# A recurrence and an MLP on one core: from hand-woven step lists to a source-level list scheduler with a shared PSUM pool and a one-function gelu

## The chip, the cores and the metric

The kernel runs on one core of one Trainium2 chip. The metric is device time in microseconds (us). The kernel before took 1344.1 us, the median of three runs (1341.94 to 1348.6).

## The reference, cut to what matters

Two parts follow each other. A recurrence over 768 steps with a 40x40 state for each of 4 x 8 heads gives `y`; its output, laid out as 3072 tokens x 320, goes through an MLP with a quick gelu. All of it is fp32, and the MLP weights arrive as fp64.

```python
for t in range(S):                                   # S = 768, D = 40
    y[:, :, t] = np.einsum('bhd,bhde->bhe', rt, state)
    Sa = np.einsum('bhde,bhe->bhd', state, at)
    state_decay = state * wt[:, :, None, :] - np.einsum('bhd,bhe->bhde', Sa, bt)
    state = state_decay + np.einsum('bhd,bhe->bhde', vt, kt)
# x: 3072 x 320, w_in: 320 x 2048, w_out: 2048 x 320
h = x @ w_in
g = h * (1.0 / (1.0 + np.exp(-1.702 * h)))
return (g @ w_out).astype(np.float32)
```

## The kernel before

The recurrence is done in chunks of 64 steps: 12 chunks x 2 pairs of batches = 24 units. In a unit a triangular system is solved by six "levels" of small matmuls, for two halves. Matmuls come in sets of four, one for each 64x64 quarter of the TensorE array (`QUARTERS` in the source; the page prints 64*64). Each chunk gives 256 tokens, and the MLP of a chunk is sixteen bursts of work: eight "ups" (into the gelu) and eight quarters of "downs". A level, with its four identity matmuls at the end, is

```python
for j in BITS:
    o = j * 168
    for h, t in QUARTERS:
        mm(ps[HALF[t], h, o + lo:o + 104], w[HALF[h], t, j, 104:], w[HALF[h], t, j, lo:104], j == 0)
    if hi == 168:
        for h, t in QUARTERS:
            mm(ps[HALF[t], h, o + 104:o + 168], w[HALF[h], t, j, :64], w[HALF[h], t, j, 104:], False)
view = ps[:, :, :336].rearrange("p h (j n) -> p h j n", n=168)
for h, t in QUARTERS:
    mm(view[HALF[t], h, :, 64:104], ident[HALF[h]], w[HALF[h], t, :, 64:104], False)
```

The order is made by hand. `weave` runs the steps of one unit's solve and slips in a share of a side list (preparation of the next unit, and the MLP of two chunks ago). PSUM, the memory that the matmuls write their results to, is held as four pairs of banks (four tiles of 128x2x512 fp32). They are split by purpose: one pair of banks for everything small, two for the levels, one for the MLP. The gelu is a sigmoid on ScalarE and a multiply on VectorE.

```python
ps_misc  = ... tile_pool(name="ps_misc",  bufs=1, space=bass.MemoryType.PSUM)
ps_solve = ... tile_pool(name="ps_solve", bufs=2, space=bass.MemoryType.PSUM)
ps_mlp   = ... tile_pool(name="ps_mlp",   bufs=1, space=bass.MemoryType.PSUM)
# [... cut ...]
nc.scalar.activation(sg, ph[:, :, :256], ACT.Sigmoid, scale=1.702)
nc.vector.tensor_mul(g, ph[:, :, :256], sg)
# [... cut ...]
if j < 0:                                   # the first two chunks: convert the weights instead
    mlp = weights[len(weights) * i // lead:len(weights) * (i + 1) // lead]
else:
    mlp = down(j) if p else up(j)           # MLP of chunk j = this one - 2
weave(solve(i), mixed(*[l for l in (side, mlp) if l]))
```

## Time and profile before

| what | value |
|---|---|
| median time | 1344.1 us |
| TensorE busy (matmul, PE) | 76% of the span |
| VectorE (DVE) / ScalarE (ACT) / GpSimd (POOL) busy | 32% / 23% / 16% |
| TensorE instructions (matmuls + weight loads) | 32416 + 32416 |
| mean granted TensorE clock (share of full speed) | 0.896 |

The lines of the three stages, the chain and the waits are in the prediction below. The first line is from the page's list of DMA queues (packets, MB, share of 16 engines' span). The second is the chain of waits by engine: the work that ended last, followed back step by step to what released it, as shares of the span. The third is one stretch of 100 us from the middle (stretch, its length, busy time with instruction counts of PE, PE weight load, DVE, ACT and POOL, granted clock, DMA share, GB/s).

```profile
q8 instruction: 254, 4.16, 1.3%
...
PE 64%; DVE 13%; ACT 8%; issue 7%; DMA 5%; POOL 3%; SPq 1%; POOLq 0%; DVEq 0%; ACTq 0%
```

TensorE has 2 x 32416 = 64832 instructions: each matmul that the kernel writes is two matmul and two weight-load records in the trace (an up, written as 20, is 40 + 40).

### The profile page before, as it was taken

The page shows a single profiled execution, that of the slowest core. Times are in us where ns is not written, and L with a number is a line of the kernel's source. Part 1 is how long each engine was busy: PE and PEld are TensorE (multiplying, and loading weights), DVE is VectorE, ACT ScalarE, POOL GpSimd, SP SyncE. Part 2 cuts the span into 40 slices and gives each one's busy share as a digit, 9 for nine tenths or more (in the row PEclk, how much of TensorE's full clock was granted, in tenths as well). Part 3 has the DMA queues.
Part 4 walks back from the last instruction along what each step waited for, and adds up shares of the span by engine and source line. Part 5 has one row for each costly group of instructions (what it writes and reads, how often), then busy time and mean ns, then how long its engine had stood idle before and what let it go on. Part 6 is the DMA issues. An engine that isn't in the chain of part 4 may idle for free.

```text
span 1348.7 us, 67403 instructions
## 1 busy us (share of the span) xinstructions
PE 1030.6 (76%) x32416; PEld 822.6 (61%) x32416; DVE 425.2 (32%) x823; ACT 313.9 (23%) x594; POOL 214.1 (16%) x238
## 2 busy tenths in 40 slices
PE   4666658787787887887887887877878878878677
PEld 3656547666666665765665665766666756665443
DVE  2676573222222322321321321322322322231110
ACT  2131212222221231231231231221321322211110
POOL 2666572001001001010010010001000100100000
PEclk9886677898997997998899898989989989899999
DMA  3233230101101101101101000110110110100000
GB/s 124 61 97 114 93 119 3 43 9 57 43 9 57 43 9 57 43 8 39 40 26 49 25 36 8 58 43 9 58 43 8 58 43 9 48 3 13 1 11 11
DMA packets 22544, 54.91 MB, mean 41 GB/s; under 512 B 2816, under 2 KB 14080, under 8 KB 22272
## 3 DMA queue, kind: packets, MB, share of 16 engines
q1 hardware_dynamic: 22272, 50.61, 11.9%
q8 instruction: 254, 4.16, 1.3%
q14 instruction: 18, 0.15, 0.0%
HBM read 46.66 MB, written 3.93 MB: 38 GB/s over the span
## 4 chain that ended last, share of the span: by engine, by line
PE 64%; DVE 13%; ACT 8%; issue 7%; DMA 5%; POOL 3%; SPq 1%; POOLq 0%; DVEq 0%; ACTq 0%
PE ps_down L530 17%; PE ps_up L512 16%; PE ps_level L94 11%; DMA in_chan<-in_chan 4%; PE ps_cum L94 3%; DVE W L318 3%; ACT sg L515 3%; PE ps_turn L94 2%; PE ps_N L94 2%; DVE g L517 2%; PE ps_y L94 2%; PE ps_saT L94 2%; PE ps_Av L94 1%; PE ps_RV L94 1%; PE ps_Z L94 1%
## 5 line engine op out<-in xcount | busy, mean ns | idle before, releaser
L512 PE MATMUL ps_up<-xT,w_in_sb 64*64 64x256 f32 x3840 | 250.0, 403 | 23.0 <-DVE g L517 20.2
L530 PE MATMUL ps_down<-w_out_sb,g 64*64 64x320 f32 x3072 | 255.0, 472 | 5.4 <-DVE g L517 2.9
L94 PE MATMUL ps_level<-W 64*64 64x64 f32 (+2 forms) x8448 | 227.5, 243 | 21.3 <-issue 10.9
L94 PEld LDWEIGHTS ps_level<-W 64*64 64x64 f32 x8448 | 209.9, 143 | 39.8 <-issue 13.1
L512 PEld LDWEIGHTS ps_up<-xT,w_in_sb 64*64 64x64 f32 x3840 | 160.9, 145 | 81.0 <-DVE g L517 26.6
L530 PEld LDWEIGHTS ps_down<-w_out_sb,g 64*64 64x64 f32 x3072 | 141.6, 149 | 76.5 <-issue 17.4
L517 DVE TENSOR_TENSOR g<-ps_up,sg 128x512 f32<-128x512 f32 x96 | 66.2, 690 | 260.6 <-ACT sg L515 260.6
L480 POOL TENSOR_TENSOR x<-y,F 64x320 f32<-64x320 f32 x24 | 20.4, 851 | 636.2 <-DVE y L475 636.0
L408 DVE COPY W<-ps_level 128x672 f32<-128x672 f32 (+1 forms) x120 | 96.0, 800 | 78.2 <-PE ps_level L94 77.8
L515 ACT ACTIVATE sg<-ps_up 128x512 f32<-128x512 f32 x96 | 57.4, 597 | 269.8 <-PE ps_up L512 269.8
L94 PE MATMUL ps_level<-W,ident 64*64 64x80 f32 x2304 | 107.5, 242 | 2.7 <-issue 2.5
L408 ACT COPY W<-ps_level 128x672 f32<-128x672 f32 (+1 forms) x120 | 81.3, 677 | 121.2 <-PE ps_level L94 117.8
L94 PEld LDWEIGHTS ps_level<-W,ident 64*64 64x64 f32 x2304 | 73.5, 143 | 3.6 <-issue 3.6
L94 PE MATMUL ps_xT<-ident,x 64*64 64x64 f32 x960 | 32.5, 262 | 37.7 <-POOL x L480 23.7
L171 POOL TENSOR_SCALAR scale<-scale 128x256 int32<-128x256 int32 (+1 forms) x36 | 47.3, 1315 | 66.1 <-DVE scale L170 65.9
L94 PEld LDWEIGHTS ps_xT<-ident,x 64*64 64x64 f32 x960 | 26.6, 168 | 44.0 <-POOL x L480 26.2
L535 ACT COPY ob<-ps_down 128x320 f32<-128x320 f32 x24 | 10.2, 426 | 182.7 <-PE ps_down L530 182.7
L278 POOL TENSOR_TENSOR ah<-in_time,F 128x320 f32<-128x320 f32 x24 | 23.4, 975 | 181.5 <-DMA in_time<-in_time 101.0
L332 POOL TENSOR_TENSOR RV<-RV,upper 128x512 f32<-128x512 f32 x24 | 30.5, 1272 | 131.8 <-ACT RV L331 131.6
L172 POOL TENSOR_SCALAR scale<-scale 128x256 int32<-128x256 int32 (+1 forms) x36 | 47.8, 1329 | 3.0
L94 PE MATMUL ps_RV<-in_chan 64*64 64x64 f32 x768 | 20.9, 262 | 33.4 <-DMA in_chan<-in_chan 31.5
L94 PE MATMUL ps_saT<-ident,sa 64*64 64x64 f32 x768 | 21.4, 257 | 28.5 <-DVE W L318 23.5
(103 smaller groups left out, 1204.1 us busy)
## 6 DMA issues: line engine op xcount, KB each, us to landing
in_time<-in_time SPq DMA_DIRECT2D x24, 800.0 KB, 5.0
in_chan<-in_chan SPq DMA_DIRECT2D x24, 512.0 KB, 6.0
raw<-in_w_in SPq DMA_DIRECT2D x40, 128.0 KB, 3.0
raw<-in_w_out SPq DMA_DIRECT2D x16, 320.0 KB, 3.0
in_w<-in_w SPq DMA_DIRECT2D x24, 160.0 KB, 6.4
out<-ob SPq DMA_DIRECT2D x48, 80.0 KB, 2.2
```

The costliest lines, as they stand in the source:

```text
L94: nc.tensor.matmul(o, lhsT, rhs, start=start, stop=True, skip_group_check=True)
L171: nc.gpsimd.tensor_scalar(scale, scale, 896.0, 0.0, ALU.subtract, ALU.max)
L172: nc.gpsimd.tensor_scalar(scale, scale, 255.0, 2.0 ** 23, ALU.min, ALU.mult)
L278: nc.gpsimd.tensor_mul(s["ah"][:, :, :D], by_head(a_b), by_head(Fs[i]))
L318: nc.vector.tensor_tensor(s["W"][b][:, :, :, o:o + 64], ps[:, :, b * 128:b * 128 + 128].rearrange("p e (f t) -> p e f t", t=64), mask.unsq ...
L332: nc.gpsimd.tensor_mul(s["RV"], s["RV"], upper8)
L408: copy(W[b][:, :, :, lo:], view[:, :, :, lo:])
L480: nc.gpsimd.tensor_mul(x[HALF[0]], y[HALF[0]], F[HALF[0]])
L512: nc.tensor.matmul(ph[HALF[h], r, :256], w_in_sb[HALF[r], k, m, h * 64:(h + 1) * 64], xTs[j][HALF[r], k, :], start=k == 0, stop=k == NK - 1)
L515: nc.scalar.activation(sg, ph[:, :, :256], ACT.Sigmoid, scale=1.702)
L517: nc.vector.tensor_mul(g, ph[:, :, :256], sg)
L530: nc.tensor.matmul(po[p][HALF[b], r, :DM], gTs[j][f // 2][HALF[r], f % 2, o:o + 64], w_out_sb[HALF[r], f, :], start=f == 0, stop=f == NF - 1)
```

## The change

The intent is to let no engine stand still while work is ready. All steps become small tasks with a rank, fixed durations and declared buffers. `Plan.order()` runs a list scheduler in the source that decides, once, the order on each engine. Four PSUM pairs form one pool. The gelu becomes one ScalarE function. Masks and multiplies leave GpSimd for VectorE, copies go to whichever of ScalarE and VectorE is free in the plan, and the weight conversion is rewritten: six VectorE operations a piece instead of five, one GpSimd operation instead of two.

```diff
+class Plan:
+    DELAY = {"PE": 330.0, "DVE": 130.0, "ACT": 130.0, "POOL": 150.0, "SP": 100.0}
+    def order(self):
+        def fits(t):
+            if t.pair is None or t.pair in held:
+                return True
+            clear = sum(p <= now for p in pairs)
+            return clear > 0 if t.most is None else clear > 1 and len(many) < t.most
+        while coming or able:
+            able.sort(key=lambda t: (t.rank, t.n))
+            # [... first task that fits on the first free engine; cut ...]
 [... cut ...]
-    ps_misc = ctx.enter_context(tc.tile_pool(name="ps_misc", bufs=1, space=bass.MemoryType.PSUM))
-    ps_solve = ctx.enter_context(tc.tile_pool(name="ps_solve", bufs=2, space=bass.MemoryType.PSUM))
-    ps_mlp = ctx.enter_context(tc.tile_pool(name="ps_mlp", bufs=1, space=bass.MemoryType.PSUM))
+    banks = ctx.enter_context(tc.tile_pool(name="banks", bufs=1, space=bass.MemoryType.PSUM))
 [... cut ...]
+        rank = 5000 + n                       # conversion of weight piece n
 [... cut ...]
-            sg = buf("sg", [128, 2, 256])
-            nc.scalar.activation(sg, ph[:, :, :256], ACT.Sigmoid, scale=1.702)
-            nc.vector.tensor_mul(g, ph[:, :, :256], sg)
+                plan.add(10000 + 100 * j + m, pe((1, 256)), part(k), ..., pair=("up", n), most=2)
+            plan.add(10000 + 100 * j + m, act(512), lambda t, n=n: nc.scalar.activation(
+                g_of(n), psum(t, "")[:, :, :256], ACT.Gelu_apprx_sigmoid), writes=[("g", n)], pair=("up", n))
 [... cut ...]
+                plan.add(10000 + 100 * j + 20 * (p + 1) + m, pe((2, 320)), part(m), ..., pair=("down", n), most=2)
```

Steps of the recurrence have ranks of about 10 per unit, so every MLP step (10000 and up) yields to every recurrence step that is ready. An MLP pair is opened only if more than one PSUM pair is clear.

## The prediction

> **What bounds the kernel now.** I read the page first: one core, a span of 1348.7 us, TensorE (PE) busy 76%, no other engine above 32%, DMA at a mean of 41 GB/s. So PE is the only candidate for a bound, but it isn't full. I then cut the span into its three stages (columns: stretch, its length, PE, PE weight load, DVE, ACT and POOL busy with instruction counts, granted PE clock, DMA share, GB/s).
>
> ```profile
> PE 1030.6 (76%) x32416; PEld 822.6 (61%) x32416; DVE 425.2 (32%) x823; ACT 313.9 (23%) x594; POOL 214.1 (16%) x238
> ...
> 0.00:236.00 236.00, 149.12 (x5256) 130.77 (x5260) 134.80 (x310) 54.06 (x105) 123.33 (x124) 0.78 0.28 87
> 236.00:1210.00 974.00, 778.56 (x25193) 628.71 (x25188) 270.81 (x484) 243.06 (x459) 88.92 (x111) 0.91 0.11 34
> 1210.00:1349.00 139.00, 102.95 (x1976) 63.12 (x1968) 19.59 (x31) 16.81 (x30) 1.85 (x3) 0.99 0.04 9
> ```
>
> The first stage converts the weights beside units 0 to 3 of the recurrence (there are 24 units, two to a chunk), the middle runs units beside the MLP of two chunks earlier, the last is mostly bare MLP. In the first, PE is idle for a third of the time and the clock is 0.78. Busy time overstates PE, since the end of each burst is counted in full. So I took from the chain of waits what bursts cost where they follow each other with no gap, and what the bare MLP looks like at the end.
>
> ```profile
> 649.46 0.73 PE ps_level L94 x40
> 650.19 0.46 PE ps_turn L94 x32
> 650.65 0.73 PE ps_level L94 x40
> 651.38 2.21 PE ps_up L512 x40
> ...
> 659.17 0.60 PE ps_level L94 x40
> 659.78 0.46 PE ps_A L94 x32
> ...
> 1321.57 2.43 PE ps_up L512 x40
> 1324.03 0.61 ACT sg L515
> 1324.66 0.70 DVE g L517
> 1325.41 8.89 PE ps_down L530 x128
> ```
>
> Packed, an up burst is 2.21 us, a quarter of a down product 8.89/4 = 2.22 us, a level 0.73 us, a transpose or score of 32 instructions 0.46 us. In the last stage each up is 3.83 us from start to start (1317.74 to 1321.57 in the same chain): 2.43 of PE, then sigmoid, multiply and hand-overs with PE still, because there is one PSUM pair for the MLP. The waits show the same disease in the middle: no single wait is big, PE stops many times for a copy out of the one "misc" pair.
>
> ```profile
> PE ps_RV L94 <- DMA in_chan<-in_chan: 31.5, 9, 4.5
> PE ps_cum L94 <- ACT logw L228: 20.9, 18, 1.2
> PE ps_saT L94 <- DVE W L318: 18.3, 19, 1.0
> PE ps_xT L94 <- POOL x L480: 17.1, 10, 2.0
> ```
>
> **The floor.** The matmuls stay the same 32416, so their packed cost is the floor. Up: 3840/40 = 96 bursts x 2.21 = 212. Down: 3072/32 = 96 x 2.2 = 211. Levels: 48 unit halves x (4 x 0.73 + 0.60 + about 0.37 for the last, which has 24 of 40 instructions) = 187. The 306 bursts of 32 (ten per unit, three more from unit 2 on) x 0.46 = 141; bridge, update and read-out at the same rate 14 + 44; the decay sums some 1.3 us a unit, 31. Sum 840 us near full clock: 423 MLP and 417 recurrence, 17.4 a unit. So 1344 holds some 500 us of idle PE and slow clock.
>
> [...] the last-stage lines show one purpose waiting while the other pairs are empty. [...] ACT 23% and DVE 32% show both have room. [...] The 597 ns sigmoid over 128x512 and the 1283 ns table loads of this trace [...] let me give the gelu 0.60 us; no run yet shows it.
>
> **The change, part by part.**
> *Gelu as one function:* removes 96 DVE multiplies (66.2 us of DVE) and from each up the 0.70 us multiply with its hand-over. On PE's path that is worth most at the end: 16 ups there x 0.74 = 12 us. Table loads stay at about one pair per chunk.
> *One pool of four pairs, MLP at most two:* up m+1 runs while the gelu of m reads. In the last stage the up falls from 3.83 to 2.2 us: 16 x 1.6 = 26 us with the gelu's 12 included, plus 6 us at the four down ends. The three pairs outside the level bursts are open to whichever transpose, score or up is ready, instead of one misc pair emptied in turn.
> *Order by readiness:* recurrence first, MLP (rank 10000) as filler, all interleaved in bursts of at most about 2 us. The recurrence may lead by up to four chunks (four xT buffers); loads go out as their buffers clear, so the in_chan wait (31.5) should shrink. The loop in one pair of batches, load 6, scale and transposes 4, A and Av 3, ahZ 1, six levels at 0.73 + 0.8 copy + 0.4 of hand-over = 12, update 1.5, comes to about 28 us a chunk, and both batch pairs run side by side; PE needs 2 x 17.4 + 35 = 70 us a chunk. So PE, not the loop, sets the pace.
> *POOL and DVE:* POOL loses x (20.4 + 24.0), RV (30.5), z (15.9) and one of two weight operations (48). DVE loses g (66) and about 3 by joining mask halves, and gains RV masks 17, z 11, x about 28 (a 511 ns and two of some 320 ns a unit, from rows of those widths), one more weight operation 13: 425 again. ACT loses the RV copies (14): 300. All on 970 us or so, under half: neither can bind outside the start.
>
> **The sum.** *Start.* Weights now cost DVE 83 + 13 = 96 us; the rest of DVE and ACT, without gelu and output, is (425 - 96 - 12 + 300 - 57 - 10)/24 = 23 us a unit. Four chunks of lead: 8 x 23 + 96 = 280 us, on two engines 140; at my guess of three quarters full 186 us, including about 25 us before the first levels. PE does 8 x 17.4 = 139 of recurrence in it and perhaps 25 of MLP (ups that have their weights): 164. *Rest.* 840 - 164 = 676 us of PE work. Best slices of before reach a clock of 0.95 to 0.98, so I choose 0.96; the filler is nearly always ready, so I choose 90% for occupancy (before: the middle stage, 80% busy even by the generous count). 676/(0.96 x 0.90) = 782. *End.* The last down's two output steps and store, 3 to 4 us. 186 + 782 + 4 = 972 us; I say 970, 28% less.
>
> **Rivals.**
> *A: the start keeps its length.* The conversion ranks behind every recurrence step on DVE, its raw buffers lie in xT slots 2 and 3, and so the bridge of chunk 2 waits for it. If four chunks with weights still take 236 us, +50: about 1020. For: first-stage DVE 135 of 236 us with POOL beside it. Against: POOL's share of the conversion halves.
> *B: the static order misfits.* The scheduler works with fixed durations in source; a late copy or DMA holds PE's queue although filler is ready behind it. Some 650 recurrence bursts with 0.2 us each would be 130 us: 1090. Against: its durations match this trace closely (source 170 + 1.03 x 512 = 697 ns, the profile's 690 for that DVE form; source 130 ns hand-over, trace lines above about 30 to 50).
> *C: PE packs as the lines above do everywhere after the first 100 us,* clock 0.98, 95%: 160 + 690/0.93 = 900.
> *D: the load loop binds.* in_time has two buffers, so the load of unit i+2 can go only after update i; with 6 us exposed per chunk, +70: 1040. I think the filler hides it.
>
> **Range and chances.** A and B push up, C down, B being the widest: 905 to 1055 eight times in ten. Even B at twice its size stays below 1317 us, so faster by over 2% has 0.97, within 2% 0.02, slower 0.01 (a mishap such as a table load at each gelu).
>
> **What would show it.** Right: PE instruction count unchanged and packed bursts at the same durations; PE busy 88 to 94% with clock 0.94 or more after some 190 us; first 190 us with PE about 75% and DVE the fullest; DVE near 425, ACT 300, POOL under 100; no DVE multiply after up and gelu about 0.60 us; the last 60 us bare MLP with ups 2.2 us apart; PE's biggest waits under 20 us each. Wrong: PE idle charged to DMA in_time (D); conversion still running at 230 us (A); clock no higher than 0.91 (then 676/(0.91 x 0.90) gives 1015); many short waits on copies totalling over 100 us after the start (B); more than some 26 table loads.

The clock is the estimate of 0.96 from the slices of before (in its middle stage the best slices of 34 us were granted 0.95 to 0.98). The 0.60 us of the gelu is an estimate from the 597 ns sigmoid. The 28 us a chunk of the loop is an estimate as well: 0.73 and 0.8 are lines of the trace, but the 0.4 us of hand-over a level is not. The lines quoted show 0.22 us for the end of a lone up burst (2.43 beside 2.21 us packed) and about 30 to 50 ns for a hand-over.

## More of the kernel before

```profile
500.00:600.00 100.00, 79.70 (x2558) 64.70 (x2550) 27.53 (x49) 24.99 (x47) 9.67 (x12) 0.90 0.11 36
```

The q8 queue brings nothing but instructions: 254 packets, 4.16 MB, 16 KB each.

In the middle of the kernel TensorE issues (2558 + 2550)/100 = 51 instructions per us.

## The result, and the profile after

The changed kernel takes 1121.0 us (four runs, 1120.24 to 1121.5), beside 1343.0 for the kernel before in the same rounds. The ratio is 0.834 (95%: 0.831 to 0.837). Ratios here are the mean time of one kernel's runs over that of the other's of the same rounds, so they are not quite the ratio of the medians. The gain is 222 us, 17%; I had predicted 970 us, and 1121 is outside my range of 905 to 1055.

From the page after: span, busy times, the instruction queue and the chain by engine.

```profile
span 1118.4 us, 67147 instructions
...
PE 903.2 (81%) x32416; PEld 825.8 (74%) x32416; DVE 332.6 (30%) x699; ACT 351.2 (31%) x648; POOL 81.4 (7%) x117
...
q8 instruction: 253, 4.15, 1.5%
...
PE 78%; issue 18%; DVE 2%; ACT 2%; POOL 0%; POOLq 0%; ACTq 0%; DVEq 0%
```

The chain now has almost nothing of DVE, ACT, POOL or DMA in it. These fell from 29% together to 4%. In their place "issue" rose from 7% to 18%: time in which TensorE waits for nothing that the profile shows. The stages (columns as above):

```profile
0.00:500.00 500.00, 335.90 (x16182) 309.14 (x16183) 231.78 (x502) 180.41 (x344) 70.65 (x98) 0.94 0.24 77
500.00:900.00 400.00, 353.48 (x12506) 313.67 (x12509) 90.30 (x175) 135.21 (x241) 10.71 (x19) 1.00 0.12 35
900.00:1119.00 219.00, 213.86 (x3736) 202.96 (x3727) 10.48 (x22) 35.58 (x63) 0.00 (x0) 1.00 0.05 12
```

Two things are to be seen. The clock is no longer the trouble (0.94, 1.00, 1.00). And half of the instructions are issued in the first 500 us at 67% PE busy, then PE is 88% busy, then 98% in a last 219 us that holds little but the MLP. Instructions per us, both kinds added: 64.7, 62.5, 34.1.

The largest waits of PE (engine, line, releaser: us in total, times, longest):

```profile
PE ps_level L194 <- issue: 82.6, 68, 5.0
PE ps_turn L194 <- issue: 16.3, 18, 2.3
PE ps_N L194 <- issue: 15.0, 12, 3.5
```

The waits for in_chan, logw, W and x that headed the list before are no longer among the large ones. A stretch of the chain in order of time (start, us, what) shows what "issue" looks like:

```profile
387.38 1.15 issue
388.53 0.69 PE ps_level L194 x25
...
390.97 1.30 issue
392.27 0.40 PE ps_level L194 x9
...
394.75 1.36 issue
396.11 0.73 PE ps_level L194 x25
...
398.58 0.10 PE ps_N L194 x4
398.68 1.38 issue
400.05 0.61 PE ps_N L194 x23
```

The stops come every 3.8 us, last 1.2 to 1.4 us, and fall into the middle of a burst: at 398.68 the same score burst is cut in two, four matmuls before the stop and 23 after it. The plan asks for a burst's operands and its PSUM pair before the first matmul, so a missing one should stop TensorE ahead of a burst, not within it. I therefore laid the arrivals of the q8 queue, from the trace's DMA records, beside the starts of TensorE's instructions:

```
block of instructions arrives | PE stands still    | PE instructions since the last stop
386.10 to 386.98              | 387.16 to 388.53   | 256
389.63 (1.31 us long)         | 390.76 to 392.27   | 256
393.49 (1.27)                 | 394.52 to 396.11   | 255
397.36 (1.23)                 | 398.46 to 400.05   | 254
401.18 (0.96)                 | 401.93 to 403.53   | 256
```

Each block is 16384 bytes, and in this stretch TensorE stops after each 256 instructions. Over the whole trace there are 150 stops above 0.8 us (from one start to the next; 10% to 90%: 0.9 to 2.1 us), 109 before 500 us, 41 from there to 900 us and none after; 93% of them lie a multiple of 256 instructions, within six, after the one before. TensorE resumes 1.38 us after the end of the last block (10% to 90%: 1.25 to 1.52). The next block starts 1.2 us after it has resumed, and takes about 1 us. That gives 3.55 to 3.9 us a block up to 900 us (medians of stretches of 100 us). In the tail blocks are 7 us apart and PE hardly stops (busy 214 of 219 us). All gaps of PE above 0.5 us, counted from start to start, sum to 246 us (PE's idle time by the profile's ends is 215 us); 160 of these 176 gaps, 234 us of them, end between 1.15 and 1.65 us after a block has landed. In the middle of the kernel before (236 to 1210 us) only 37 of 270 such gaps do, 32 of 269 us, little more than the tenth that chance would give; there blocks are 4.0 to 4.8 us apart (medians of stretches of 100 us).

The trace also tells how far the supply runs ahead. At each landing I counted the blocks landed so far, less the instructions started so far in units of 256. In the trace after this stays between -0.73 and 0.67 from the first block to the last, and between 0.18 and 0.67 in the tail, where a block is used up in 7 us. No reserve builds up even where there is time for it.

So I form theory **F**: TensorE executes faster, in the recurrence, than its instructions are supplied. The supply gives 256 in about 3.75 us, 68 per us. A level (40 matmuls and 40 loads in 0.73 us) asks for 110 per us, a transpose burst (32 and 32 in 0.46 us) for 139; an up (40 and 40 in 2.21 us) asks for only 36. The rival theory **W** says that PE waits for work in another form: the late weight conversion, the static order, copies and hand-overs, which the profile just fails to name. A second rival is the array itself: the packed time of the matmuls. The expectations below use these letters.

### The profile page after: what moved, and what is told of

Same layout as the page of the kernel before. It is cut to its first block, busy times and chain, and to the rows that moved or that the text cites. A ratio compares the mean times of both kernels' runs of the same rounds, so it can differ in the third digit from the quotient of the medians. Undisturbed runs are those within 1.5% of the kernel's fastest.

```text
span 1118.4 us, 67147 instructions
## 1 busy us (share of the span) xinstructions
PE 903.2 (81%) x32416; PEld 825.8 (74%) x32416; DVE 332.6 (30%) x699; ACT 351.2 (31%) x648; POOL 81.4 (7%) x117
## 4 chain that ended last, share of the span: by engine, by line
PE 78%; issue 18%; DVE 2%; ACT 2%; POOL 0%; POOLq 0%; ACTq 0%; DVEq 0%
PE ps_level L194 19%; PE ps_up L714 19%; PE ps_down L733 18%; PE ps_turn L194 3%; PE ps_N L194 2%; PE ps_y L194 2%; PE ps_cum L194 2%; PE ps_Z L194 2%; PE ps_xT L194 1%; PE ps_saT L194 1%; PE ps_A L194 1%; PE ps_RV L194 1%; PE ps_M L194 1%; PE ps_Av L194 1%; PE ps_rz L194 1%
## 5 line engine op out<-in xcount | busy, mean ns | idle before, releaser
L714 PE MATMUL ps_up<-xT,w_in_sb 64*64 64x256 f32 x3840 | 226.5, 377 | 7.2 <-issue 5.2
L714 PEld LDWEIGHTS ps_up<-xT,w_in_sb 64*64 64x64 f32 x3840 | 192.2, 133 | 18.1 <-issue 7.3
L588 ACT COPY W<-ps_level 128x672 f32<-128x672 f32 (+1 forms) x206 | 138.0, 678 | 211.2 <-PE ps_level L194 202.2
L733 PEld LDWEIGHTS ps_down<-w_out_sb,g 64*64 64x64 f32 x3072 | 167.9, 134 | 24.2 <-issue 3.0
L720 ACT ACTIVATE g<-ps_up 128x512 f32<-128x512 f32 x96 | 57.3, 597 | 137.1 <-PE ps_up L714 136.7
L305 POOL TENSOR_SCALAR scale<-scale 128x256 f32<-128x256 f32 (+1 forms) x36 | 41.4, 1161 | 235.1 <-DVE scale L301 235.1
L588 DVE COPY W<-ps_level 128x672 f32<-128x672 f32 (+1 forms) x34 | 26.3, 785 | 74.6 <-PE ps_level L194 66.4
L194 PEld LDWEIGHTS ps_y<-kh,RV 64*64 64x64 f32 x768 | 27.7, 143 | 5.8 <-issue 2.6
L194 PE MATMUL ps_y<-bh,M 64*64 64x40 f32 x768 | 29.1, 235 | 2.2 <-issue 2.2
L194 PE MATMUL ps_Z<-sa,bh 64*64 64x40 f32 x704 | 25.2, 226 | 6.9 <-issue 6.9
```

The lines of the kernel that those rows point to most:

```text
L194: nc.tensor.matmul(o, lhsT, rhs, start=start, stop=True, skip_group_check=True)
L305: nc.gpsimd.tensor_scalar(scale().bitcast(FP32), scale().bitcast(FP32), low, high, ALU.max, ALU.min)
L588: copy(t.engine)(W_of(s + 1)[:, :, b, :, lo:], view[:, :, :, lo:])
L714: nc.tensor.matmul(ph[HALF[h], r, :256], w_in_sb[HALF[r], k, m, h * 64:(h + 1) * 64], xT_of(j)[HALF[r], k, :], start=k == 0, stop=k == NK - 1)
L720: plan.add(10000 + 100 * j + m, act(512), lambda t, n=n: nc.scalar.activation(g_of(n), psum(t, "")[:, :, :256], ACT.Gelu_apprx_sigmoid), w ...
L733: nc.tensor.matmul(po[HALF[b], r, :DM], g_of(j * NM + m)[HALF[r], f % 2, o:o + 64], w_out_sb[HALF[r], f, :], start=f == 0, stop=f == NF - 1)
```

## The experiments

Twelve kernels ran; "after" is 1121.0 us.

### weights_first: is it the late weight conversion?

My rival A had a sign that did show: conversion was still running at 230 us. The work on the tile `scale` (DVE, POOL busy, clock, DMA share, GB/s) after:

```profile
300.00:350.00 50.00, 12.05 (x30) 6.36 (x5) 1.00 0.21 68
350.00:400.00 50.00, 0.00 (x0) 0.00 (x0) 1.00 0.12 38
```

The first up starts at 273 us. The edit puts the conversion ahead of everything:

```diff
-        rank = 5000 + n
+        rank = -50 + n * 0.1
```

> The weight conversion gets the highest rank instead of one behind the whole recurrence, so it should end near 180 us instead of 345. Rival A (the prediction's: the slow conversion is what stretches the start and keeps the MLP out): at least 50 us faster, 1070 or less. F: PE's rate of instructions in front stays at 60 to 67 per us and the total within 2%, possibly up to 25 us slower because DVE delays the first units.

```profile
200.00:500.00 300.00, 0.00 (x0) 0.00 (x0) 0.99 0.17 53
```

Conversion now ends before 200 us, yet the time is 1119.3 us (ratio to the kernel before 0.835; that of after is 0.834). Over the first 500 us it issues 64.4 instructions per us against 64.7. The sign was right and the cause wrong: on its own, weights that come earlier are worth nothing. The MLP still ranks last, and the ups of the first 500 us take 24 us of PE where they took 25.

### wide_turn: array time that brings no instructions

If F holds, more work per instruction is free where PE would stop anyway. The transposes get a moving operand of 128 columns instead of 64 (the identity twice); the second copy is ignored. The count of matmuls stays.

```diff
+    def turn_wide(ps, src, r, c, col):
+        mm(ps[HALF[c], r, col * 128:col * 128 + 128], src, ident2[HALF[r]], col == 0)
 [... the three turns and saT use it, and copies read [:64] of each 128 ...]
```

> The counterpart of the added small matmuls: more array time, no more instructions. The transposes of ah, kh, bh and of the solution use a moving operand of 128 columns (the identity twice) in place of 64; the copies take the first half. 96 bursts, each longer by an estimated 0.41 us (64 more columns in 8 steps of two, at the rate of the packed bursts), 40 us of array time in all, order kept, result correct. F: where instructions are late the array time is free, so at most +12 us, 1133. W or a PE bound by its array: +40 us or near it, since these bursts are on the recurrence's path: 1150 to 1165.

One of the four rows after, and then the same row of this run (count, busy us, mean ns, idle ahead of it):

```profile
L194 PE MATMUL ps_turn<-ident,ah 64*64 64x64 f32 x768 | 18.5, 225 | 6.1 <-issue 4.4 <-DVE ah L443 1.0 <-DVE ob L744 0.6
```

```profile
L194 PE MATMUL ps_turn<-ident,ah 64*64 64x128 f32 x768 | 29.3, 283 | 2.2 <-issue 0.8 <-DVE ob L752 0.6 <-ACT G L389 0.6
```

The four rows together went from 76.6 to 120.1 us of busy time, and the kernel took 1119.6 us, 1 us less. Some 43 us of added array time (41 by PE's total, 903.2 to 943.9) cost nothing, and the "issue" idle ahead of the row shrank. The array is not the bound in the recurrence.

### no_ident: fewer instructions

The four identity matmuls at the end of a level are dropped (a wrong result: relative error 0.036). They are 4608 TensorE instructions, 18 blocks.

```diff
-                for h, q in QUARTERS:
-                    mm(view[HALF[q], h, :, 64:104], ident[HALF[h]], w[HALF[h], q, :, 64:104], False)
```

> Wrong result on purpose: the four matmuls in each level that add x through the identity are left out, 4608 PE instructions, 18 blocks, array time 288 x 0.14 = 40 us. The copies, their waits and the order stay. F: most of 18 x 3.75 = 67 us, so -50 to -67, 1055 to 1070. If array time is the bound: -40, 1081. If the copies and waits are: less than 20 us.

Measured: 1055.2 us, 66 less, ratio 0.785. F's 18 x 3.75 is 67. An estimate by array time gave 40, and W less than 20.

### idle_mm_front and before_idle_mm: instructions without work, and a trap

In the first, the decay sums of the first eight units get 128 matmuls of two columns each, 16 blocks in all, which go nowhere. In the second, the same stand in units 8 to 15 of the kernel before.

```diff
+            for _ in range(32 if i < 8 else 0):
+                for b, e in QUARTERS:
+                    mm(ps[HALF[e], b, 488:490], ident[HALF[b]], halves[HALF[b]], False)
```

> Theory F (PE's instruction supply): in the changed kernel's trace PE stops every 255 or 256 instructions while a 16 KB block of its program is fetched, one block per 3.4 to 3.9 us. This run adds 128 small matmuls (two columns, 512 PE instructions) to each of the first eight units, 4096 instructions or 16 blocks, in the stage where PE gets only 61 to 67 instructions per us; nothing reads their result and the order of everything else is kept. F: 16 x 3.75 = about +60 us, 1181. Rival W (PE waits for copies, PSUM pairs or weights there): the added matmuls cost at most their own array time, 1024 matmuls x 29 ns (a burst of 16 matmuls takes 0.46 us) = +30 us, and less where they fall into idle time: 1121 to 1151.

> The kernel before with 128 small matmuls in the decay sums of units 8 to 15, in the middle stage, where PE takes about 51 instructions per us and most of its stops are waits for other engines. F says that there the blocks of instructions come in time, so the added ones cost their array time and no more: about +30 us, 1.022 times the kernel before, not the +60 they cost in the changed kernel's front. If instructions were the bound before as well: +60, 1.045.

Measured: 1180.0 us, which is 59 more, as F said; but the control on the kernel before also took 59 us more (1404.4 against 1345.1, ratio 1.045), twice what I had expected. The trace of the control shows something else at work. One dense burst, stretch and columns as in the stages:

```profile
368.30:375.20 6.90, 6.90 (x273) 6.90 (x269) 0.00 (x0) 0.00 (x0) 0.00 (x0) 0.50 0.02 5
```

PE is busy all the time, at a clock of 0.50. Three of the eight bursts run so, 6.85 us each without a stop, about twice what I had reckoned. In the stretch of another, 500.40 to 507.20 us, the mean clock is 0.71, and PE is busy 6.40 of 6.80 us. What sets the clock there no run shows. Clock and supply cannot be told apart here. Both runs are thus confounded, and I take neither as evidence for F.

### front_spread and before_spread: the same without the trap

Here the instructions are of the ordinary width (64 columns) and are spread over the levels, 12 to each: 1152 matmuls, 4608 instructions, 18 blocks; in units 0 to 7 of after, and in units 8 to 15 of before.

```diff
+                for _ in range(3 if i < 8 else 0):
+                    for h, q in QUARTERS:
+                        mm(ps[HALF[q], h, 336:400], ident[HALF[h]], ident[HALF[h]], False)
```

> The added matmuls in front again, because the run of the kernel before with added matmuls showed that a dense burst of two-column matmuls runs at half clock (0.50, 6.8 us a burst), so that array time alone could explain the +59 us of the first front run. Now 12 matmuls of 64 columns per level of units 0 to 7, 1152 matmuls, 4608 PE instructions or 18 blocks, spread over 96 level bursts, the mirror of the run that left out the identity matmuls. Array time 288 sets x 0.116 = 33 us. F: up to 18 x 3.75 = +67 us, 1175 to 1188. Array bound: +33, 1154. Copies and waits the bound: +20 or less.

> The same added matmuls in the levels of units 8 to 15 of the kernel before, its middle stage at 51 instructions per us. F: on average the blocks come in time there, so array time, +33 us or 1.025 times the kernel before, a little more where a level burst follows another. If the supply of instructions bound that stage as well: +67, 1.05.

front_spread: 1199.3 us, 78 more (ratio 0.892). That is above even F's 67 and far from the array's 33; the 11 us over stay open. (PE's total busy time rose by 47 us, 903.2 to 950.5, so 33 is too low for the array, but 78 is above that as well.) The first 500 us keep their rate, 64.3 per us, although each burst has become longer:

```profile
0.00:500.00 500.00, 328.93 (x16066) 305.34 (x16070) 205.95 (x464) 158.42 (x299) 67.82 (x94) 0.94 0.23 70
```

before_spread: 1392.1 us, 48 more than the 1344.3 of its rounds (ratio 1.036, 1.031 to 1.042): between the 33 of the array, which I had expected, and the 67 of the supply. The traces agree: of the gaps above 0.5 us in the middle, those that end 1.15 to 1.65 us after a block has landed grew from 37 of 270 (32 us) to 60 of 260 (65 us). So the kernel before, with these added, is limited by supply in part too, though its average of 51 per us is below the rate. This fits a supply that runs little ahead (by the count above, -0.73 to 0.67 blocks in the trace after, and -0.71 to 0.88 in that of before), so that a dense stretch meets it even where the average does not.

### idle_mm_tail: the two-column instructions where the supply has room

```diff
+                    for _ in range(8 if j >= 8 and k == NK - 1 else 0):
+                        for r, h in QUARTERS:
+                            mm(ph[HALF[h], r, 256:258], ident[HALF[r]], halves[HALF[r]], False)
```

> The same 1024 small matmuls, 4096 PE instructions, but in the last four chunks' up products, where PE runs bare MLP at 34 instructions per us and the blocks of its program come in time. F and W agree here: array time alone, 1024 x 29 ns = about +30 us, 1151. What counts is the difference from the run with the same matmuls in front: F says front costs twice the tail, W says front costs the same or less.

1148.1 us, 27 more by the medians and 31 by the ratio (0.857), as expected from array time; the clock is 1.00 from 900 to 1000 us. Together with front_spread it says that in this kernel an instruction costs its supply in the front (78 us for 18 blocks) and its array time in the tail (27 to 31 us for 16). The pair is not exact: the matmuls here have two columns and those of front_spread 64, and no run put the 64-column ones in the tail.

### mix: move no work, only the order

If the front lacks instructions and the tail has them to spare, the MLP should not come last. It gets ranks among the recurrence's, so that slow-rate bursts (36 per us) stand between fast-rate ones.

```diff
-            return clear > 0 if t.most is None else clear > 1 and len(many) < t.most
+            return clear > 0 if t.most is None else clear > 0 and len(many) < t.most
-                plan.add(10000 + 100 * j + m, pe((1, 256)), part(k), ...)
+                plan.add(20 * (j + 1) + 10 + m * 1.2, pe((1, 256)), part(k), ...)
-                plan.add(10000 + 100 * j + 20 * (p + 1) + m, pe((2, 320)), part(m), ...)
+                plan.add(20 * (j + 1) + 10 + 10 + 5 * p + m * 0.6, pe((2, 320)), part(m), ...)
 [... the gelu's and the output's ranks likewise; cut ...]
```

> Only the order changes: the MLP tasks of chunk j are ranked among the recurrence tasks of a chunk or two later instead of behind all, and an MLP pair may open when one pair is clear. Same instructions, same scheduler durations, same PE array work. F: the MLP's bursts, which need 34 instructions per us, are spread between the recurrence's, which need over 100, so fewer blocks are late; an estimate from 253 blocks x 3.75 us = 949 plus some 90 us of start and unevenness: 1040, with the bare MLP tail shorter than 100 us and PE instructions per us near 64 throughout. Rival W: no gain beyond 2%, since the filler was ready anyway; the time stays in 1100 to 1140.

1037.1 us, 84 less (ratio 0.774), with the same instructions:

```profile
0.00:500.00 500.00, 409.59 (x15348) 354.28 (x15352) 202.23 (x461) 177.70 (x319) 64.64 (x88) 0.96 0.23 72
500.00:900.00 400.00, 358.43 (x13268) 311.42 (x13260) 102.92 (x192) 144.83 (x261) 16.25 (x25) 1.00 0.14 41
900.00:1043.00 143.00, 132.02 (x3812) 113.54 (x3804) 26.09 (x50) 39.09 (x70) 3.09 (x4) 1.00 0.06 16
```

Compare the first line with that of after. The front issues even fewer instructions, 61.4 per us, but PE is busy 410 us of 500 instead of 336: each block holds more work. The bare MLP at the end, after the last matmul of the recurrence, shrinks from 155 us (958 to 1113) to 52 (986 to 1038).

### mix2: a better version

The conversion goes early as well, PE's durations in the plan get a floor of 150 ns, where it was 116, for each set of four matmuls (so that the plan charges small ones more), and the MLP's ranks move forward by ten; `clear > 1` stays as in after.

```diff
-        return {"PE": sum(n * 2 * max(58.0, cols / 1.2 + 3) for n, cols in sets)}
+        return {"PE": sum(n * max(150.0, 2 * (cols / 1.2 + 3)) for n, cols in sets)}
-        rank = 5000 + n
+        rank = n * 1.0
 [... ranks as in mix, without the "+ 10" ...]
```

> A step beyond the mixed order: weights earlier as well, and the scheduler charges a short burst for its instructions (150 ns a set of four matmuls where it charged 116). Same instructions. F: a few us to 20 us below the first mixed order's 1037: 1015 to 1037. If the instruction supply were not what the mixed order eased, charging for it should not help: 1037 or slower.

1021.7 us (1019.3 to 1024.7, ratio 0.760), correct, and the fastest of all kernels here: 9% below after.

```profile
0.00:500.00 500.00, 425.10 (x15776) 374.42 (x15780) 184.64 (x431) 196.30 (x359) 67.42 (x91) 0.97 0.23 73
500.00:900.00 400.00, 362.59 (x13356) 314.49 (x13352) 86.15 (x163) 157.07 (x290) 16.25 (x25) 1.00 0.14 43
900.00:1020.00 120.00, 109.45 (x3292) 95.84 (x3284) 19.64 (x38) 38.98 (x71) 2.73 (x4) 0.99 0.05 10
```

It runs at 63, 67 and 55 instructions per us, and its gaps above 0.5 us, from start to start, are down from 246 us to 129. Which of its edits gave the 15 us over mix was not taken apart.

### two_op_gelu and before_gelu: the part that is the gelu

In the first, after gets the two operations back; in the second, before gets the one function alone.

```diff
-                g_of(n), psum(t, "")[:, :, :256], ACT.Gelu_apprx_sigmoid), writes=[("g", n)], ...)
+                g_of(n), psum(t, "")[:, :, :256], ACT.Sigmoid, scale=1.702), writes=[("sg", n)], ...)
+            plan.add(10000 + 100 * j + m, dve(512), lambda t, n=n: nc.vector.tensor_mul(
+                g_of(n), psum(t, "")[:, :, :256], g_of(n)), reads=[("sg", n)], writes=[("g", n)], ...)
```

```diff
-            sg = buf("sg", [128, 2, 256])
-            nc.scalar.activation(sg, ph[:, :, :256], ACT.Sigmoid, scale=1.702)
-            nc.vector.tensor_mul(g, ph[:, :, :256], sg)
+            nc.scalar.activation(g, ph[:, :, :256], ACT.Gelu_apprx_sigmoid)
```

> Undoes one part: the gelu is a sigmoid on ScalarE and a multiply on VectorE again, in the changed kernel's schedule (which takes the extra step into account). The prediction gave the gelu 12 us at the end; with two pairs for the MLP the multiply should lie beside the next up product. F and the trace (DVE busy 6 to 10% in the tail): within 1%, 1115 to 1130. If the gelu carried the gain: 20 us slower or more.

> The kernel before with the gelu as one ScalarE function and nothing else. By the prediction's arithmetic the 16 ups of the last stage each lose 0.72 us of multiply and hand-over with PE still: -12 us; in the middle the multiply frees the one MLP pair 0.7 us earlier at 80 ups, part of which PE was waiting for: another 5 to 15 us. So 1320 to 1332, about -1%.

two_op_gelu: 1129.4 us, 8 more (ratio 0.840, whose interval, 0.835 to 0.844, overlaps that of after). before_gelu: 1315.1 us against 1345.1 (ratio 0.980, 0.975 to 0.985), 27 us by the ratio, a little more than the 13 to 25 that I had expected. So the gelu is worth about 27 us to a kernel with one MLP pair. Where other pairs cover it, it is worth 7 or so at most, which is not clear of the noise. Of the 222 us, some 195 or more thus come from the rest of the change; no run takes order, pool and the moves between engines apart.

## Why the prediction was wrong

**The step that failed is "The floor".** I wrote that "their packed cost is the floor", 840 us of array time. There is a second floor that I did not look for: the instructions themselves. 64832/256 = 253 blocks at about 3.75 us are 949 us, an estimate from the blocks and the period of the trace after, and it is above the 840. Nor is the average the worst of it. The supply runs hardly ahead (-0.73 to 0.67 blocks), so it has to be met locally, and my rule for the order did the opposite: recurrence first, MLP as filler for idle slots. A stop for instructions is no slot that a later task could fill, since that task's instructions, as far as the trace tells, come through the same queue (q8 brought 253 blocks, and 64832/256 is 253). The evidence: 43 us of added array time were free (wide_turn), 18 blocks fewer gave 66 us (no_ident), 18 more in the front cost 78 (front_spread), and the order alone gave 84 (mix). The 500-us fronts shown here all issue 61 to 65 instructions per us, while PE's busy time in them goes from 329 us (front_spread) to 425 (mix2).

**The start.** I gave 164 us of packed work 186 us. If I count bursts by my own packed durations in the trace after, 156 us of work are done by 300 us and 220 by 400; 164 are reached near 310. I had taken ScalarE and VectorE for the limit; it was 64.7 instructions per us. The durations of the packed bursts that I used were right for single bursts. In the middle of the kernel before, only 37 of 270 gaps end just after a block has landed; no run isolates what the supply did there while the packed bursts ran.

**The rest.** I divided 676 us by 0.96 (clock) and 0.90 (occupancy). The clock was better than that, 1.00 from 500 us on. Occupancy was not 0.90 but, from 310 us to the end, 676/808 = 0.84, and unevenly: starving in front, 98% in the tail. 310 + 808 is the span. By blocks, (16182 + 16183 + 12506 + 12509)/256 = 224 in the first 900 us at 3.75 us are 840 us, and the tail of 219 us is packed: 1059. The other 59 us (the first loads, and the waits that remain) no run takes apart.

**The tail.** This held. The chain at the end shows ups back to back:

```profile
1010.38 17.27 PE ps_up L714 x320
1027.64 17.23 PE ps_down L733 x256
```

320/40 = 8 ups in 17.27 us are 2.16 us each (predicted 2.2, before 3.83). By my count of packed work (the prediction's durations, summed over the trace) the last 96 us of it took 139 us before and take about 100 now: 39 us gained, against my 32. Of the rest of the gain, by the same count, about 54 us lie in the first 92 us of work (236 us before, 182 after) and about 138 in the work between.

**The gelu.** One function takes the time of the sigmoid, 0.60 us as predicted:

```profile
L720 ACT ACTIVATE g<-ps_up 128x512 f32<-128x512 f32 x96 | 57.3, 597 | 137.1 <-PE ps_up L714 136.7
```

**DVE, ACT, POOL.** POOL at 81 us was as predicted (under 100). DVE is at 333 us (425 predicted) and ACT at 351 (300): the plan gave more of the free copies to ScalarE than I assumed, and the rewritten conversion is cheaper than my 96 us. As said there, neither could bind.

**The rivals.** A had its listed sign and not its effect (weights_first). B's listed sign, many short waits on copies, did not show: PE's waits are "issue". (Its sum was off as well: 970 + 130 is 1100, not 1090.) C's assumption of 95% packing everywhere is what the supply did not allow (a level asks for 110 instructions per us, and the front got 64.7). D's sign, PE waiting for in_time, did not appear; no DMA is among PE's largest waits. A, B and D were about data, engines and buffers; none of the four was about how TensorE gets its instructions, and this is why the range missed. The sign was in the page all along: 254 packets of instructions, 110 instructions per us inside a level, and "issue" at 7% of the chain.

What stays open: why a block takes 3.75 us. The trace shows the order (the block lands, PE resumes 1.38 us later, and the next block starts 1.2 us after that) but not what happens in these two intervals. Also open are the 11 us by which front_spread overshot.

## What to carry to other kernels

Where a kernel is made of many small fp32 matmuls, as here, divide TensorE's instructions by the time, stage by stage and burst by burst, and compare it with what the instruction queue is seen to deliver (here 61 to 67 per us up to 900 us in after, mix and mix2) before calling packed array time a floor. In this case the mark was stops of like length (1.2 to 1.4 us in the stretch shown) every 256 instructions, in the middle of bursts and charged to "issue". What helped here was fewer instructions (66 us for 18 blocks, no_ident) and an order that puts bursts of large matmuls between bursts of small ones, rather than leaving the large ones as filler for the end (84 us, mix). More columns to each instruction cost nothing: 43 us of added array time, 1 us less (wide_turn).
